# Keys and probabilities turned by VectorE in 32x32 blocks in place of TensorE transposes, in a decoding kernel on one core

## The chip, the core and the metric

The kernel runs on one core of a Trainium2 chip. The metric is the device time of one execution in microseconds (us). The engines that matter: TensorE (PE; its weight loads are PEld), VectorE (DVE), ScalarE (ACT), GpSimd (POOL), and SyncE (SP), whose queue issues nearly all DMA transfers to 16 DMA engines.

## The reference

One decoding step for 8 sequences, width 512. x is normalised (layernorm); the result goes two ways.

```python
q = (xn @ wq).reshape(8, 1, 32, 128)            # 32 query heads, 8 key heads (4 queries each)
k, v = last 2048 positions of k_cache, v_cache  # each batch and key head: 2048 x 128 bf16
p = softmax(q . k * 128 ** -0.5)
s = (p . v).reshape(8, 4096) @ wo
g = silu((sigmoid(xn @ w_gate) * (xn @ w_up)) @ w_down)   # 512 -> 1792 -> 512
out = x + s * g
```

Weights are some 14 MB, keys and values of the window 67 MB; each byte is used once or by four queries.

## The kernel before, in words

All large tensors go through nine slots in SBUF of 16 KB per partition. A list of requests in a fixed order is served first in, first out: `free` gives a slot back and `pump` issues the next transfer on SP's queue. The order is gate, up and down weights (`wd_sb` with 11 rows of w_down on each partition, and a small tile `side` with the 384 rows left, laid on few partitions), wq in two halves, then the cache: one tile for 4 key heads of one batch (2,048 KB, `k_sb` or `v_sb`; a partition holds one head's 64 consecutive positions), the value tiles three places behind the key tiles, and at the end wo in four pieces (16, 10, 4 and 2 of 32 rows). A batch has two key tiles and two value tiles.

The head of the kernel (L194 to L440) computes layernorm, gate and up products, the down product and g, and the queries: `q_ps`, transposed by TensorE (L380), copied to `qm_sb` (L385).

Then a loop over the batches, each in 16 half steps, interleaved by hand through a table `tasks`:

- `k_transposes` (L449): 8 TensorE transposes of 128x128 into PSUM (L456; the identity `perm` also orders the columns by head), then one VectorE copy of 128x1024 to `kT_sb` (L461). 16 of these per batch.
- `scores` (L467): four matmuls, one per head, side by side in strips of 32 columns of the array (L474).
- `row_max` (L485): one VectorE maximum per row of scores (L487), four exponentials with their sums (L494) to `p_buf`. A row holds a quarter of one query's scores.
- `stat_rows`, `factor`, `spread` (L505 to L556): the rows' maxima and sums are turned to one partition, combined into a factor per row, and turned back.
- `p_transposes` (L558): 16 TensorE transposes of the probabilities (L563), two VectorE copies (L568).
- `value` (L574): probabilities times values into `o_ps`; up to batch 4 in the form 128x512, after that 128x256. `values_some` puts them two batches behind the keys.
- `combine`, `normalise`, `turn` (L600 to L639): scaling, and the way back to one column per batch in `oP_sb`.

Behind the loop stands the tail for the last batches, and then the output product: 32 rows of wo, four narrow matmuls each (L706), then two VectorE operations and four small stores. A key slot is freed at its last transpose, a value slot at its last `value`.

What waits on what: SP's queue waits for slots; TensorE takes its instructions in the order written, so a matmul that waits for a tile holds all behind it.

Of the kernel before, what the change touches and what calls it, by code (L numbers as in the profile page):

```python
# [10 lines left out]
def kernel(  # L11
# [30 lines left out]
    CH = CU // 2  # L42
    NU = NQ * NJ
    NR = NU * rep
# [19 lines left out]
        tc.tile_pool(name="ps_t", bufs=4, space=bass.MemoryType.PSUM)  # L64
# [5 lines left out]
        tc.tile_pool(name="ps_o", bufs=1, space=bass.MemoryType.PSUM)  # L70
# [40 lines left out]
    LOW, SF = (5, 5, 3, 3), 15  # L111
    MID, SM = 9, 4
    SP = 4 * max(LOW)
    M_AT = 32
    MP = 4 * MID
    MT = 11
    m0 = MT * P
    m1 = m0 + SF * sum(LOW)
    assert m1 + SM * MP == F
    side = {}  # L120

    def want_side(w, q, at, count, rows, base, of):
        def f(tag=None):
            if tag:
                t = slots.tile([P, SF, w.shape[1]], bf16, name="side", tag=tag)
                nc.gpsimd.memzero(t[:M_AT])  # L126
                side["t"] = t
                rows_of[("side", 0)] = (t, tag)
                for r in range(SF):
                    weights[("wd_sb", MT + r)] = t[: M_AT + MP if r < SM else SP, r]  # L130
            q0.dma_start(  # L131
                out=side["t"][at + q : at + q + 4 * (count - 1) + 1 : 4, :rows].rearrange(
                    "p s n -> p (s n)"
                ),
                in_=w[base : base + of * count * rows, :].rearrange(
                    "(p q s) n -> q p (s n)", q=of, s=rows
                )[q % of],
            )

        todo.append((not side, f))  # L140
        side["asked"] = True
# [32 lines left out]
    sides = []  # L174
    for q in range(4):
        sides.append((q, 0, LOW[q], SF, m0 + q // 2 * 2 * LOW[0] * SF, 2))
        sides.append((q, M_AT, MID, SM, m1, 4))
# [13 lines left out]
    for t0, t1 in ((0, 16), (16, 26), (26, 30), (30, RT)):  # L191
# [13 lines left out]
    perm = consts.tile([P, P], bf16, name="perm")  # L205
    nc.gpsimd.tensor_copy(  # L206
        out=perm[:].rearrange("k (l p) -> k l p", l=G),
        in_=ident[:].rearrange("k (p l) -> k l p", l=G),
    )


    x_f = work.tile([B, D], f32, name="x_f")
    nc.vector.tensor_copy(out=x_f[:], in_=x_bf[:])
    stats = work.tile([B, nc.vector.BN_STATS_DIM], f32, name="stats")
    nc.vector.bn_stats(out=stats[:], in_=x_f[:])
# [7 lines left out]
    xn_bf = work.tile([B, D], bf16, name="xn_bf")  # L223
    nc.vector.tensor_scalar(  # L224
        out=xn_bf[:],
        in0=x_f[:],
# [7 lines left out]
    for kt in range(KT):  # L234
        nc.tensor.transpose(  # L235
            out=xnT_ps[:, kt, :],
            in_=xn_bf[:].rearrange("b (p kt) -> b kt p", kt=KT)[:, kt, :],
            identity=ident[:B, :B],
        )
    xnT_sb = work.tile([P, KT, Z], bf16, name="xnT_sb")  # L240
    nc.vector.memzero(xnT_sb[:])
    nc.vector.tensor_copy(out=xnT_sb[:, :, :B], in_=xnT_ps[:])  # L242
# [5 lines left out]
    h_side = work.tile([B, SF, M_AT + MP], bf16, name="h_side")  # L248
# [4 lines left out]
    M0 = Z - rep  # L253
    qm_sb = work.tile([P, B, Hkv, M0 + Z], bf16, name="qm_sb")
    nc.gpsimd.memzero(qm_sb[:])
    p_buf = [work.tile([P, PG, G, CU], bf16, name=f"p_buf{i}") for i in range(2)]
    for t in p_buf:
        nc.gpsimd.memzero(t[:])
# [16 lines left out]
    for k in range(F // FC):  # L275
        g_ps = ps_t.tile([B, FC], f32, name="g_ps", tag="t")
        for kt in range(KT):
            nc.tensor.matmul(  # L278
                g_ps[:],
                lhsT=xnT_sb[:, kt, :B],  # L280
# [9 lines left out]
    h_bf = ktpool.tile([P, CU * P], bf16, name="h_bf", tag="kT")  # L290
    for k in range(F // FC):
        u_ps = ps_t.tile([B, FC], f32, name="u_ps", tag="t")
        for kt in range(KT):
            nc.tensor.matmul(  # L294
                u_ps[:],
                lhsT=xnT_sb[:, kt, :B],
# [12 lines left out]
    for h in range(2):  # L309
# [10 lines left out]
    nc.gpsimd.tensor_copy(  # L320
        out=h_side[:, :SM, M_AT:],
        in_=h_bf[:B, m1:F].rearrange("b (p t) -> b t p", t=SM),
    )
    cuts = [h_bf[:B, :m0].rearrange("b (p t) -> b t p", t=MT)[:, t] for t in range(MT)]
    rows = [P] * MT + [M_AT + MP] * SM + [SP] * (SF - SM)
    cuts += [h_side[:, t, : rows[MT + t]] for t in range(SF)]
# [5 lines left out]
    for k, t0, t1 in ((M_AT + MP, MT, MT + SM), (SP, MT + SM, MT + SF)):  # L332
        nc.scalar.copy(out=hT_sb[:k, t0:t1, :B], in_=hT_ps[:k, t0:t1])
# [13 lines left out]
    q_ps = [ps_t.tile([P, D], f32, name="q_ps", tag="t") for _ in range(2)]  # L347
    for kt in range(KT):
        for e in range(2):
            for g in range(G):  # L350
                c0 = (G * e + g) * D
                nc.tensor.matmul(  # L352
                    q_ps[e][Z * g : Z * (g + 1), :],
                    lhsT=xnT_sb[:, kt, :],
                    rhs=weights[("wq_sb", kt)][:, c0 : c0 + D],
                    start=(kt == 0),
                    stop=(kt == KT - 1),
                    tile_position=(0, Z * g),
                    skip_group_check=True,
                )  # L360
# [14 lines left out]
    for e in range(2):  # L375
        q_bf = ktpool.tile([P, D], bf16, name="q_bf", tag="kT")
        nc.scalar.mul(out=q_bf[:], in_=q_ps[e][:], mul=scale)
        qT_ps = ps_t.tile([P, rep, G, Z], bf16, name="qT_ps", tag="t")
        for r in range(rep):
            nc.tensor.transpose(  # L380
                out=qT_ps[:, r].rearrange("p g z -> p (g z)"),
                in_=q_bf[:, r * Dh : (r + 1) * Dh],
                identity=ident[:],
            )
        nc.vector.tensor_copy(  # L385
            out=qm_sb[:, :, G * e : G * (e + 1), M0 : M0 + rep].rearrange(
                "p b g r -> p r g b"
            ),
            in_=qT_ps[:, :, :, :B],
        )  # L390
# [13 lines left out]
    for j in range(NB):  # L404
# [12 lines left out]
    Hh = G * rep  # L417
    turn_rows = consts.tile([P, P], bf16, name="turn_rows")
    nc.gpsimd.tensor_copy(
        out=turn_rows[:].rearrange("k (x l r) -> k x l r", x=NU, l=G),  # L420
        in_=ident[:].rearrange("k (l x r) -> k x l r", x=NU, l=G),
    )
    sel_e = consts.tile([P, 2, Hq], f32, name="sel_e")
    for e in range(2):
        nc.vector.reduce_sum(
            out=sel_e[:, e, :].rearrange("k (i h) -> k i h", i=NQ),
            in_=ident_f[:].rearrange(
                "k (i m e h) -> k e i h m", i=NQ, m=NJ // 2, e=2
            )[:, e],
            axis=AX.X,  # L430
        )

    o_ps = ps_o.tile([P, NJ, Dh], f32, name="o_ps")
    sel_j = ident_f[:].rearrange("k (i j h) -> k j i h", i=NQ, j=NJ)
    m_ps = ps_m.tile([P, 512], f32, name="m_ps", tag="m")
    top_ps = m_ps[0:1, 0:P]
    sum_ps = m_ps[0:1, P : 2 * P]
    fac_ps = m_ps[:, 2 * P : 2 * P + 1]
# [3 lines left out]
    kT = {}  # L442
    s_ps = {}
    pT = {}
    st = {}
    row = {}
    fac = {}

    def k_transposes(b, u, h):  # L449
        i, j = u // NJ, u % NJ  # L450
        k_sb = k_tiles[(b, i)][0]
        if h == 0:
            kT[(b, u)] = ktpool.tile([P, CU, P], bf16, name="kT_sb", tag="kT")
        kT_ps = ps_t.tile([P, CH, P], bf16, name="kT_ps", tag="t")
        for c in range(CH):
            nc.tensor.transpose(  # L456
                out=kT_ps[:, c, :],
                in_=k_sb[:, j * CU + h * CH + c, :],
                identity=perm[:],
            )  # L460
        nc.vector.tensor_copy(  # L461
            out=kT[(b, u)][:, h * CH : (h + 1) * CH, :], in_=kT_ps[:]
        )
        if j == NJ - 1 and h == 1:
            free(k_tiles.pop((b, i)))

    def scores(b, u):  # L467
        i, j = u // NJ, u % NJ
        if u == 0:
            s_ps[b] = ps_s.tile([P, CU * PG], f32, name="s_ps", tag="s")  # L470
        t = kT.pop((b, u))
        o = M0 - rep * u
        for l in range(G):
            nc.tensor.matmul(  # L474
                s_ps[b][NR * l : NR * (l + 1), :],
                lhsT=qm_sb[:, b, i * G + l, o : o + Z],
                rhs=t[:, :, PG * l : PG * (l + 1)],
                start=(u == 0),
                stop=(u == NU - 1),
                tile_position=(0, NR * l),  # L480
                skip_group_check=True,
            )


    def row_max(b):  # L485
        st[b] = small.tile([P, 1], f32, name="st")
        nc.vector.tensor_reduce(  # L487
            out=st[b][:], in_=s_ps[b][:], axis=AX.X, op=ALU.max, negate=True
        )
        sums = small.tile([P, 1], f32, name="sums")  # L490
        s = s_ps.pop(b)
        for l in range(G):
            rows = slice(NR * l, NR * (l + 1))
            nc.scalar.activation(  # L494
                out=p_buf[b % 2][rows, :, l, :],
                in_=s[rows, :].rearrange("k (c p) -> k p c", p=PG),
                func=AF.Exp,
                bias=st[b][rows, :],
                accum_out=sums[rows, :],
            )  # L500
        fac[b] = sums

    LI = G * NQ

    def stat_rows(b):  # L505
        nc.tensor.transpose(out=top_ps, in_=st.pop(b)[:], identity=ident_f[:])
        nc.tensor.transpose(out=sum_ps, in_=fac.pop(b)[:], identity=ident_f[:])
        rv = top_ps.rearrange("o (a j r) -> o a j r", a=LI, j=NJ)
        top = small.tile([1, LI, rep], f32, name="top")
        nc.vector.tensor_reduce(  # L510
# [244 lines left out]
```

## Time and profile before

| what | value |
|---|---|
| median of 3 runs | 199.12 us (199.09 to 199.34) |
| profiled execution | 199.33 us |
| its span | 197.5 us, 4796 instructions |
| PE busy | 157.4 us (80%), 2112 matmuls |
| DVE busy | 125.4 us (63%), 245 instructions |
| ACT busy | 40.7 us (21%) |
| POOL busy | 11.0 us (6%) |
| DMA | 81.32 MB, mean 412 GB/s |
| key transposes L456 on PE | 72.6 us |
| their copies L461 on DVE | 84.2 us |

The span is what the profiler saw between the first and the last instruction; the profiled execution's own time is 1.8 us longer. Busy shares are averages over the whole span. In the page's rows of digits, each digit is the busy share of one fortieth of the span in tenths, and 9 means 90% or more. In a group's row stand the line, the engine, the operation, output and input with their shapes, how often, busy time in all, the mean in ns, and the idle time before with what ended it.

### The profile page before, as it was taken

Reading aid. Unit: us, or ns where it says so; the run is one execution under the profiler, and the core shown is the slowest. Engines: PE = TensorE matmul, PEld = TensorE weight load, DVE = VectorE, ACT = ScalarE, POOL = GpSimd, SP = SyncE. Lnnn points to the kernel's source line nnn. Section 1 sums busy time; section 2 is a strip of 40 time slices with the busy share of each in tenths; the row PEclk is TensorE's granted clock in tenths of the full one; section 3 lists DMA queues with packets and bytes.
Section 4 is the critical chain, followed back from the end, with each engine's and each line's share of the span. In section 5 each row is a group of like instructions: output and inputs, shape, how many; then the busy total and the mean of one; then the engine's idle time right before and its main releaser. Section 6 shows DMA issues by size and latency. Waiting matters only on the chain.

```text
span 197.5 us, 4796 instructions
## 1 busy us (share of the span) xinstructions
PE 157.4 (80%) x2112; PEld 103.1 (52%) x2112; DVE 125.4 (63%) x245; ACT 40.7 (21%) x95; POOL 11.0 (6%) x22
## 2 busy tenths in 40 slices
PE   0089559999788898799979987999799979976733
PEld 0034325776664565466545654566466556655531
DVE  4623106999797696679666965796669658935201
ACT  0522022006306001600160016001600160071000
POOL 8910200000000000000000000000000000000000
PEclk9999859999999999999999999999999999999975
DMA  6999999999999999999999999999999999999980
GB/s 205 424 440 435 431 434 435 425 425 431 423 425 425 438 428 435 431 425 428 422 433 431 435 425 433 428 418 428 428 438 431 428 428 431 428 423 425 428 366 21
DMA packets 6396, 81.32 MB, mean 412 GB/s; under 512 B 812, under 2 KB 820, under 8 KB 1624
## 3 DMA queue, kind: packets, MB, share of 16 engines
q1 hardware_dynamic: 6328, 81.01, 96.6%
q8 instruction: 16, 0.26, 0.5%
q10 hardware_dynamic: 48, 0.01, 0.0%
q14 instruction: 4, 0.03, 0.0%
HBM read 81.01 MB, written 0.01 MB: 410 GB/s over the span
## 4 chain that ended last, share of the span: by engine, by line
DMA 73%; PE 22%; POOL 3%; SPq 0%; issue 0%; DVE 0%; POOLq 0%
DMA v_sb<-in_A_v_cache_dram 46%; DMA wo_sb<-in_A_wo_dram 14%; PE kT_ps L456 11%; DMA wq_sb<-in_A_wq_dram 7%; DMA k_sb<-in_A_k_cache_dram 6%; PE o_ps L584 4%; PE s_ps L474 3%; POOL side L126 2%; PE m_ps L614 1%; PE fin_ps L706 1%; PE pT_ps L563 1%; SPq L131 0%; POOL perm L206 0%; POOL hT_sb L245 0%; DVE prod L717 0%
## 5 line engine op out<-in xcount | busy, mean ns | idle before, releaser
L461 DVE COPY kT_sb<-kT_ps 128x1024 bf16<-128x1024 bf16 x128 | 84.2, 683 | 28.9 <-PE kT_ps L456 25.0
L456 PE MATMUL kT_ps<-perm,k_sb 128*128 128x128 bf16 x1024 | 72.6, 220 | 3.7 <-DMA k_sb<-in_A_k_cache_dram 3.7
L456 PEld LDWEIGHTS <-k_sb 128*128 128x128 bf16 x1024 | 58.8, 98 | 26.1 <-issue 16.8
L584 PE MATMUL o_ps<-v_sb,pT_sb 128*32 128x256 bf16 (+1 forms) x352 | 36.5, 327 | 9.0 <-DMA v_sb<-in_A_v_cache_dram 7.6
L474 PE MATMUL s_ps<-kT_sb,qm_sb 128*32 128x512 bf16 x256 | 25.6, 389 | 1.3 <-DVE kT_sb L461 1.1
L494 ACT ACTIVATE p_buf<-s_ps,st 32x512 bf16<-32x512 f32 x32 | 21.7, 679 | 15.4 <-DVE st L487 15.1
L584 PEld LDWEIGHTS <-pT_sb 128*32 128x32 bf16 (+1 forms) x352 | 12.3, 101 | 21.7 <-issue 19.7
L604 ACT ACTIVATE o_sb<-o_ps,fac 128x512 f32<-128x512 f32 (+1 forms) x8 | 4.9, 608 | 60.9 <-PE o_ps L584 60.9
L568 DVE COPY pT_sb<-pT_ps 128x1024 bf16<-128x1024 bf16 x16 | 10.8, 676 | 1.8 <-PE pT_ps L563 1.8
L474 PEld LDWEIGHTS <-qm_sb 128*32 128x32 bf16 x256 | 7.0, 93 | 8.0 <-issue 1.3
L563 PE MATMUL pT_ps<-turn_rows,p_buf 128*128 128x128 bf16 x128 | 10.7, 227 | 0.0
L563 PEld LDWEIGHTS <-p_buf 128*128 128x128 bf16 x128 | 9.4, 149 | 0.2 <-issue 0.2
L521 ACT ACTIVATE w_row<-w 1x128 f32<-1x128 f32 x8 | 2.5, 309 | 30.6 <-DVE w L514 30.6
L235 PE MATMUL xnT_ps<-ident,xn_bf 8*128 8x8 bf16 x4 | 0.3, 176 | 10.6 <-DVE xn_bf L224 10.6
L385 DVE COPY qm_sb<-qT_ps 128x128 bf16<-128x128 bf16 x2 | 1.4, 881 | 8.7 <-PE qT_ps L380 8.7
L301 DVE TENSOR_TENSOR h_bf<-sig,u_ps 8x448 bf16<-8x448 f32 x4 | 2.4, 608 | 6.6 <-PE u_ps L294 6.1
L278 PE MATMUL g_ps<-wg_sb,xnT_sb 128*8 128x448 bf16 x16 | 5.7, 544 | 0.3 <-DVE xnT_sb L242 0.3
L494 ACT ACTIVATION_READ_ACCUMULATOR p_buf<-s_ps,st 32x1 f32 x32 | 5.9, 184 | 0.0
L706 PE MATMUL fin_ps<-wo_sb,oP_sb 128*32 128x128 bf16 x128 | 3.3, 263 | 3.1 <-DMA wo_sb<-in_A_wo_dram 3.1
L487 DVE TENSOR_REDUCE st<-s_ps 128x1 f32<-128x512 f32 x8 | 5.4, 681 | 0.5 <-PE s_ps L474 0.5
L235 PEld LDWEIGHTS <-xn_bf 8*128 8x128 bf16 x4 | 0.2, 117 | 10.6 <-DVE xn_bf L224 10.6
L352 PE MATMUL q_ps<-wq_sb,xnT_sb 128*32 128x512 bf16 x32 | 3.1, 526 | 3.2 <-DMA wq_sb<-in_A_wq_dram 3.2
(88 smaller groups left out, 92.0 us busy)
## 6 DMA issues: line engine op xcount, KB each, us to landing
k_sb<-in_A_k_cache_dram SPq DMA_DIRECT2D x16, 2048.0 KB
v_sb<-in_A_v_cache_dram SPq DMA_DIRECT2D x16, 2048.0 KB
wq_sb<-in_A_wq_dram SPq DMA_DIRECT2D x2, 2048.0 KB
wo_sb<-in_A_wo_dram SPq DMA_DIRECT2D x1, 2048.0 KB
wg_sb<-in_B_w_gate_dram SPq DMA_DIRECT2D x2, 896.0 KB
wu_sb<-in_B_w_up_dram SPq DMA_DIRECT2D x2, 896.0 KB
wd_sb<-in_B_w_down_dram SPq DMA_DIRECT2D x1, 1408.0 KB
wo_sb<-in_A_wo_dram SPq DMA_DIRECT2D x1, 1280.0 KB
```

Of the source, the lines that this page charges most:

```text
L126: nc.gpsimd.memzero(t[:M_AT])
L278: nc.tensor.matmul(g_ps[:], lhsT=xnT_sb[:, kt, :B], rhs=weights[("wg_sb", kt)][:, k * FC : (k + 1) * FC], start=(kt == 0), stop=(kt == KT ...
L456: nc.tensor.transpose(out=kT_ps[:, c, :], in_=k_sb[:, j * CU + h * CH + c, :], identity=perm[:],)
L461: nc.vector.tensor_copy(out=kT[(b, u)][:, h * CH : (h + 1) * CH, :], in_=kT_ps[:])
L474: nc.tensor.matmul(s_ps[b][NR * l : NR * (l + 1), :], lhsT=qm_sb[:, b, i * G + l, o : o + Z], rhs=t[:, :, PG * l : PG * (l + 1)], start=(u ...
L487: nc.vector.tensor_reduce(out=st[b][:], in_=s_ps[b][:], axis=AX.X, op=ALU.max, negate=True)
L494: nc.scalar.activation(out=p_buf[b % 2][rows, :, l, :], in_=s[rows, :].rearrange("k (c p) -> k p c", p=PG), func=AF.Exp, bias=st[b][rows, ...
L563: nc.tensor.transpose(out=pT_ps[:, c, :], in_=p_buf[b % 2][:, :, :, h * CH + c].rearrange("k p l -> k (p l)"), identity=turn_rows[:],)
L568: nc.vector.tensor_copy(out=pT[b][:, h * CH : (h + 1) * CH, :], in_=pT_ps[:])
L584: nc.tensor.matmul(o_ps[r] if b < WIDE else o_ps[r, 0:2], lhsT=pT[b][:, c, r], rhs=x, start=(c == 0), stop=(c == CU - 1), tile_position=(0 ...
L604: nc.scalar.activation(out=o[:, :n], in_=o_ps[:, :n], func=AF.Copy, scale=fac.pop(b)[:])
L706: nc.tensor.matmul(fin_ps[Z * j : Z * (j + 1), :], lhsT=oP_sb[:, t, :], rhs=weights[("wo_sb", t)][:, j * P : (j + 1) * P], start=(t == 0), ...
```

## The change

- Keys: TensorE's transposes and the copies out of PSUM go. `k_turn` lets VectorE transpose a quarter of a key tile in place, in blocks of 32x32 pairs of bf16 (seen as 4-byte elements), and writes each block so that the eight pairs of one head stand together. 8 turns per batch in place of 16 copies.
- Scores: `q_wide` holds the queries spread over a 128-row pattern with zeros (filled by GpSimd in `widen` for every batch, with two buffers). 16 matmuls of full height, 512 columns, per key tile; keys are read with a step of one pair. A row now belongs to a query and a part of the positions. The key tile is freed after its scores.
- Softmax: `row_max` transposes the rows' maxima to one partition, `head_max` takes one maximum for each query and spreads it back by a matmul; four exponentials over all 128 rows, each with a mask that leaves one head; `factor` is one matmul, one sum and one reciprocal.
- Probabilities: turned by VectorE (`p_turn`), from `p_buf` to `pT_sb`.
- Values: 16 matmuls of 64 rows by 512 columns per value tile, all batches alike; two buffers of `o_ps`.
- The queries' projection uses the whole array, and VectorE turns the queries.
- The down weights: 13 rows on each partition, `side` holds 128 rows in pieces of 4 KB.
- The output product: the first 16 rows of wo in wide matmuls of 512 columns, copied by ScalarE and added with `fold` before row 26; the rest as before.

The core of the diff:

```diff
-    def k_transposes(b, u, h):
...
-        for c in range(CH):
-            nc.tensor.transpose(
-                out=kT_ps[:, c, :],
-                in_=k_sb[:, j * CU + h * CH + c, :],
-                identity=perm[:],
-            )
-        nc.vector.tensor_copy(
-            out=kT[(b, u)][:, h * CH : (h + 1) * CH, :], in_=kT_ps[:]
-        )
+    def k_turn(b, s):
+        i, j = s // NJ, s % NJ
+        x = (
+            k_tiles[(b, i)][0][:, j * CU : (j + 1) * CU, :]
+            .rearrange("p c d -> p (c d)")
+            .bitcast(f32)
+        )
+        nc.vector.transpose(
+            out=x.rearrange("p (c l h) -> p c h l", l=G, h=2 * NA), in_=x
+        )
...
+    def scores(b, i):
...
+        for n in range(NW // NQ):
+            j, l, e = n // (2 * G), n // 2 % G, n % 2
+            o = (i * (NW // NQ) + n) * P + M0 - NL * i - rep * l
+            nc.tensor.matmul(
+                s_ps[b][:],
+                lhsT=q_wide[b % 2][:, o : o + P],
+                rhs=k[:, j, l, e],
...
+        free(k_tiles.pop((b, i)))
...
+    def exps(b):
...
+        for l in range(G):
+            nc.scalar.activation(
+                out=p_buf[b][:, :, :, l, :],
+                in_=s[:].rearrange("k (c e) h -> k c h e", e=2),
+                func=AF.Exp,
+                bias=bias[:, l : l + 1],
+                scale=mask[:, l : l + 1],
+                accum_out=sums[b][:, l : l + 1],
+            )
+
+    def p_turn(b):
+        pT[b] = ppool.tile([P, NQ, CT // 2, NL, 2], bf16, name="pT_sb")
+        nc.vector.transpose(
...
-    LOW, SF = (5, 5, 3, 3), 15
-    MID, SM = 9, 4
+    LOW, SF, SH = (5, 5, 3, 3), 8, 4
...
-    MT = 11
+    MT = 13
...
     for b in range(B):
+        tasks = {s: [] for s in range(NS)}
         if b >= 1:
+            tasks[0].append(lambda: scores(b - 1, 1))
+            tasks[1].append(lambda: row_max(b - 1))
+            tasks[2].append(lambda: head_max(b - 1))
+            tasks[2].append(lambda: exps(b - 1))
+            tasks[6].append(lambda: p_turn(b - 1))
+            tasks[6].append(lambda: factor(b - 1))
+        tasks[0].append(lambda: widen(b))
+        tasks[4].append(lambda: scores(b, 0))
...
+        for s in range(NS):
+            k_turn(b, s)
             for f in tasks[s]:
                 f()
...
     scores(last, 1)
     combine(last - 2)
     row_max(last)
+    values(last - 1, 0, 4)
+    head_max(last)
+    exps(last)
     normalise(last - 2)
+    values(last - 1, 4, NN)
+    turn(last - 2)
     combine(last - 1)
+    p_turn(last)
+    factor(last)
...
+    RG = 16
+    f_ps = ps_t.tile([P, D], f32, name="f_ps", tag="t")
+    for t in range(RG):
+        g = slice(Z * (t % G), Z * (t % G + 1))
+        nc.tensor.matmul(
+            f_ps[g, :],
+            lhsT=oP_sb[:, t, :],
+            rhs=weights[("wo_sb", t)],
...
+    nc.scalar.copy(out=f_sb[:], in_=f_ps[:])
+    for t in range(RG, RT):
+        if t == 26:
+            fold(fin_ps, f_sb, False, False)
```

The whole program has 4,091 instructions on TensorE's queue before and 1,464 after.

## The prediction

> **What bounds the kernel now.** I read the slices first, then the transfer queues, the chain, the groups of instructions, and last the end of the span in windows and in order of time.
>
> ```profile
> PE   0089559999788898799979987999799979976733
> DVE  4623106999797696679666965796669658935201
> DMA  6999999999999999999999999999999999999980
> q1 hardware_dynamic: 6328, 81.01, 96.6%
> q8 instruction: 16, 0.26, 0.5%
> DMA 73%; PE 22%; POOL 3%; SPq 0%; issue 0%; DVE 0%; POOLq 0%
> ```
>
> The DMA row is 9 from the second slice to the last but one: 81.01 MB move at some 428 GB/s from about 3 us to 191 us, whatever the engines do. The chain agrees (DMA 73%). So an engine's saving counts only where it changes when the stream ends, what follows the stream, or where an engine falls so far behind that slots come free late. One cache tile (2,048 KB) takes 2.097 MB / 428 GB/s = 4.9 us, a batch (four tiles) 19.6 us; that is the pace every engine must hold. The end, in windows (columns: length, PE, PEld, DVE, ACT, POOL busy, clock, DMA share, GB/s):
>
> ```profile
> 188.00:190.00 2.00, 1.08 (x64) 1.02 (x65) 0.03 (x1) 0.00 (x0) 0.00 (x0) 1.00 1.02 430
> 190.00:191.00 1.00, 0.00 (x0) 0.00 (x0) 0.00 (x0) 0.00 (x0) 0.00 (x0) 0.63 0.77 320
> 191.00:192.00 1.00, 0.14 (x8) 0.14 (x11) 0.00 (x0) 0.00 (x0) 0.00 (x0) 0.50 0.86 342
> 192.00:193.00 1.00, 1.00 (x40) 0.92 (x33) 0.00 (x0) 0.00 (x0) 0.00 (x0) 0.50 0.56 217
> ```
>
> The same in order of time:
>
> ```profile
> 188.81 1.08 PE L706 MATMUL fin_ps<-wo_sb,oP_sb 128*32 128x128 bf16 x64 [1.12 <-DMA wo_sb<-in_A_wo_dram]
> 191.86 2.28 PE L706 MATMUL fin_ps<-wo_sb,oP_sb 128*32 128x128 bf16 x64 [1.97 <-DMA wo_sb<-in_A_wo_dram]
> 194.19 0.29 DVE L717 TENSOR_TENSOR prod<-gg_sb,fin_ps 128x128 f32<-128x128 f32 x1 [6.16 <-PE fin_ps L706]
> ```
>
> The share falls raggedly from 190 us: some of the 16 DMA engines are done while others work to 193.2 us. PE waited for wo at 188.81 and 191.86, at a granted clock of 0.50 the second time; matmuls end at 194.1.
>
> **The stream.** Bytes stay: wd grows from 1,408 to 1,664 KB, side shrinks from 384 KB (2 x 75, 4 x 36, 2 x 45) to 128. What goes is code: in the built order of instructions PE has 4,091 rows before and 1,464 after. The 16 instruction packets above are 0.5% of 16 engines' span, 0.005 x 16 x 197.5 = 15.8 us, some 1 us each; 16 for 4,091 rows makes 6 for 1,464. Ten fewer save 10 us / 16 = 0.6 us per DMA engine: last landing 192.6 instead of 193.2. Which engine carries which packet and side row decides the ragged edge; the windows show some 1 us lost there, so I allow 0.6 us either way.
>
> **Slots.** A key slot is freed after the scores instead of after the transposes, half a tile later; a value slot comes free one or two eighths of a batch earlier. Counting the requests against nine slots, a transfer's slot is free some 15 to 20 us before the queue reaches it (key tile 6 takes the slot of key tile 0, free near 39 us, and is due near 69). Hidden; it costs only if an engine falls 15 us behind.
>
> **VectorE per batch.** Removed: 16 copies L461, 2 copies L568, seven small row operations. Added: 8 turns of 128x1024 4-byte elements, one turn of P, a maximum over 512 elements on one partition, small ones.
>
> ```profile
> L461 DVE COPY kT_sb<-kT_ps 128x1024 bf16<-128x1024 bf16 x128 | 84.2, 683 | 28.9 <-PE kT_ps L456 25.0 <-PE m_ps L632 3.4
> L487 DVE TENSOR_REDUCE st<-s_ps 128x1 f32<-128x512 f32 x8 | 5.4, 681 | 0.5 <-PE s_ps L474 0.5
> L639 DVE CAST oP_sb<-m_ps 128x32 bf16<-128x32 f32 x7 | 2.0, 292 | 0.6 <-PE m_ps L632 0.6
> L556 DVE COPY fac<-m_ps 128x1 f32<-128x1 f32 x8 | 1.1, 138 | 0.6 <-PE m_ps L550 0.6
> ```
>
> No turn of this kind is in the trace. L487 against L556 gives (681 - 138) / 511 = 1.06 ns per 4-byte element, so a turn at that pace is 1024 x 1.06 + 0.1 = 1.2 us. The other end is L639: it writes 2-byte elements 64 bytes apart and takes (292 - 138) / 31 = 5.0 ns per element; the key turn writes 4-byte words 32 bytes apart, so at worst 1024 x 5.0 + 0.1 = 5.2 us. Nothing excludes either end. I take 1.2 us: L639 writes half words, the turn whole ones, and L331, which writes runs of 16 bytes at 64-byte steps, pays nothing (88 elements, 202 ns). Per batch 8 x 1.2 + 1.2 + 0.68 + 0.65 + five small ones 1.0 = 13.1 us, under 19.6.
>
> [...]
>
> **TensorE per batch.** Gone: 128 key transposes (72.6 us in all) and 16 of P (10.7). Scores become 32 full-height 512-column matmuls, one after the other; the nearest row is L294, 16 of 448 columns in 3.19 us, 0.2 each, 0.23 for 512: 7.3 us. Values: 32 of the 128*64 form, 26.8 / 160 = 0.167 each: 5.3 us. With some 1 us of small ones 13.6 us, under 19.6. The moving keys are read with 4-byte steps, of which no row tells; the bounds are 0.23 and twice that (21 us per batch, too slow); I take 0.23, since every 512-column row here lies nearer to it.
>
> **ScalarE and GpSimd.** Exponentials stay 4 per batch over 512 columns: L494 (0.68 + 0.18, one each 0.79 us in the timeline), 3.2 us. They now write pairs, 4 bytes, 16 bytes apart: between 0.79 and, at 5.0 ns per pair, 256 x 5.0 + 0.35 = 1.6 us each. I take 0.79. GpSimd spreads the queries, 4 copies of at most 0.47 us (L206) per batch, beside everything.
>
> **The tail.** Here compute meets the stream. The last key tile is there at 164.5 us, V tiles 13, 14, 15 near 174.1, 179.0, 183.9 (188.8 less 4.9 each). Four turns to 169.3; scores 3.7 to 173.0; maximum 0.7; PE does four steps of values(6), which need V 13, to 175.4; head maximum and bias to 175.9; exponentials 3.2 to 179.1; turn of P 1.2 to 180.3; value(7,0) 16 x 0.23 to 184.0; normalise 0.6; value(7,1) 3.7 to 188.3 (before: 185.9); combine 0.7 to 189.0; normalise to turn 1.65, as before, to 190.6; 16 wide output matmuls, four at a time at 0.33 (L474), 1.3 to 191.9; 40 narrow ones at 1.08 / 64 = 0.017, 0.7, to 192.6; fold 0.43 (L337) to 193.0; 24 narrow ones 0.4 to 193.4. The stream's own end: 192.6 + 0.5 to the waiting PE + 0.15 = 193.3. Both give 193.4 in place of 194.1: 0.7 us less. The clock fell in the window in which PE stood idle (0.63); with the change PE does not stand idle there, so I take full clock; at half clock (the 2.28 against the 1.08 us above) the last 64 steps cost 1.2 us more.
>
> **Sum.** The profiled execution took 199.33 us, its span is 197.5, and the median of the runs is 199.12. 199.33 - 0.7 = 198.6; taken from the median 198.4. The tail has no margin, so I keep the upper value: **198.6 us**.
>
> **Rivals.**
> 1. Scattered writes bind VectorE. Place: the key turn. The first can start at 32.5 us, and 60 turns and seven batches of 3.5 us of other work must be done when the last tile lands: 32.5 + 60x + 24.5 = 164.5, x = 1.8 us. From there each 0.1 us costs 6.4 us. At L639's pace (5.2 us): 32.5 + 64 x 5.2 + 24.5 + 27 of tail = 417 us; at twice the contiguous pace (2.3 us) 231. For: L639 and L385 (128 scattered elements, 0.88 us). Against: both are half-word writes. Chance 0.14.
> 2. The tail's compute comes out late: exponentials at 1.6 us put 3.2 us ahead of value(7,0), of which 0.1 us is hidden, or the clock stays at 0.50. End at 194.6 to 196.5 in place of 194.1; 199.8 to 201.7 us. For: no slack in the sum. Against: wide rows of ACT are all 0.59 to 0.69 us. Chance 0.20.
> 3. It does nothing: the code's packets were not on the last DMA engine, or the new side rows are. The stream ends at 193.2: 199.1 us. Chance 0.16.
> 4. Forecast: 197.8 to 198.9, chance 0.50.
>
> What a measurement can tell from no change is about 0.2% (0.4 us). Faster: 4 but its upper edge, with the luckier part of 3, 0.50; same 0.17; slower 0.33. The range is 197.8 to 201.8: it leaves out rival 1, whose bounds reach to 417, and little below.
>
> **What would show it.** DMA row of 9 throughout and q8 with about 6 packets: the stream step. A key turn at 1.2 us on VectorE: right; over 1.8 us and a DMA row with holes: rival 1. Exponentials at 0.8 or 1.6 us, and whether PE's last matmuls wait for wo_sb or for oP_sb: rival 2. A ragged end as long as now: rival 3.

## The result, and the profile after

The changed kernel took 238.56 us (median of 4 runs, 237.07 to 238.97) against 199.13 us (199.09 to 199.34) for the kernel before in the same session: a ratio of 1.1964, 95% interval 1.1912 to 1.2016. The forecast was 198.6 us, in a range of 197.8 to 201.8. The profiled execution took 238.57 us, its span is 236.8 us. Here and below, medians and ranges hold all executions of a kernel, while ratios and their intervals leave out those that took over 1.5% longer than its fastest.

The slices of the span after (PE, DVE, the granted TensorE clock, DMA), the queue of the code, and the chain's shares by engine:

```profile
PE   0098940862861994985499559955995599578974
DVE  5614049998999988849594959496949684623000
PEclk9999995697799798598759875987598759889997
DMA  6999999999999999999999999599849994500000
q8 instruction: 6, 0.10, 0.1%
PE 56%; DVE 38%; issue 2%; ACT 1%; DMA 1%; DVEq 0%; ACTq 0%
```

Before, the chain was 73% DMA and the DMA row was full to the end. Now DMA holds 1% of the chain, and its row has holes from the 26th slice on: slots come free late. No engine is at 9 throughout in its place. PE shows 9955, DVE 9594, over and over, and the clock falls in every round (9875): a pattern with a period of four slices, 24 us. The chain of waits, in order of time (start, length, engine, tile, line, count), shows one such round:

```profile
108.97 5.32 PE s_ps L478 x16
114.31 0.69 DVE st L489
115.01 1.89 DVE k_sb L465
...
118.42 1.88 PE m_ps L598 x8
120.30 5.40 PE s_ps L478 x16
125.69 1.85 PE o_ps L570 x16
...
127.70 0.30 DVE oP_sb L623
128.00 1.81 DVE k_sb L465
129.81 1.06 DVE pT_sb L543
...
131.12 1.89 DVE k_sb L465
...
133.05 5.32 PE s_ps L478 x16
```

From one score row to the same row of the next batch it is 133.05 - 108.97 = 24.1 us, where the stream delivers a batch in 19.6. In this round VectorE is busy 18.1 us and TensorE 17.6: each has room, but they take turns. Two places in the written order show in the chain. `row_max` (L489) stands at half step 1, right behind `scores` of the same tile at half step 0; VectorE waits there, 12.5 us in all, with all its turns queued behind. And `turn` of an older batch (its copy L623) stands at half step 5: its matmul is on TensorE's queue behind `scores` of half step 4 and the values, so VectorE waits again, 20.9 us in all, while the next `scores` wait for the turns behind that copy. A third is smaller: `normalise` (L598) waits on TensorE for the bias of `head_max` (2.5 us in all), ahead of the next `scores`. Now the three groups of instructions that the forecast priced:

```profile
L465 DVE STREAM_TRANSPOSE k_sb<-k_sb 128x1024 f32<-128x1024 f32 x64 | 121.4, 1971 | 0.0
L478 PE MATMUL s_ps<-k_sb,q_wide 128*128 128x512 bf16 x256 | 80.0, 479 | 32.4 <-DVE k_sb L465 21.3
L532 ACT ACTIVATE p_buf<-s_ps,bias,mask 128x512 bf16<-128x512 f32 x32 | 25.3, 812 | 99.3 <-DVE bias L516 99.3
```

A key turn takes 1.97 us, not 1.2; 0.77 us more, 64 times. A score matmul takes 5.32 / 16 = 0.33 us in the ring, against the 0.23 assumed. The exponentials start 0.78 us after each other, against the 0.79 assumed. The windows of one round show at which clock the matmuls ran (length, PE, PEld, DVE, ACT, POOL, clock, DMA share, GB/s):

```profile
106.00:109.00 3.00, 0.30 (x5) 0.12 (x2) 2.97 (x5) 0.69 (x1) 0.00 (x0) 1.00 1.01 431
109.00:114.00 5.00, 5.00 (x16) 1.81 (x15) 3.54 (x2) 0.00 (x0) 0.00 (x0) 0.66 1.00 429
```

TensorE stood nearly idle for 3 us, and the next 5 us of scores were granted 0.66 of the clock: in steps of 1 us, 1.00 from 109 us, 0.65 from 110, and 0.50 from 111 to 113. Behind the loop there is a long tail: the last key turn ends at 204.9 us, and 32 us of mostly serial work follow, in which DMA moves next to nothing.

### The profile page after: what moved, and what is told of

Same layout as the page of the kernel before. It is cut to its first block, busy times and chain, and to the rows that moved or that the text cites. A ratio compares the mean times of both kernels' runs of the same rounds, so it can differ in the third digit from the quotient of the medians.

```text
span 236.8 us, 2156 instructions
## 1 busy us (share of the span) xinstructions
PE 158.9 (67%) x833; PEld 73.8 (31%) x834; DVE 157.9 (67%) x151; ACT 40.7 (17%) x87; POOL 21.2 (9%) x53
## 4 chain that ended last, share of the span: by engine, by line
PE 56%; DVE 38%; issue 2%; ACT 1%; DMA 1%; DVEq 0%; ACTq 0%
PE s_ps L478 29%; DVE k_sb L465 24%; PE o_ps L570 9%; PE m_ps L598 5%; DVE pT_sb L543 3%; PE q_ps L337 3%; PE g_ps L268 3%; DVE x_f L202 2%; DVE st L489 2%; PE m_ps L508 2%; DVE low L499 1%; PE u_ps L284 1%; DVE oP_sb L623 1%; DMA x_bf<-in_A_x_dram 1%; PE f_ps L681 1%
## 5 line engine op out<-in xcount | busy, mean ns | idle before, releaser
L465 DVE STREAM_TRANSPOSE k_sb<-k_sb 128x1024 f32<-128x1024 f32 x64 | 121.4, 1971 | 0.0
L478 PE MATMUL s_ps<-k_sb,q_wide 128*128 128x512 bf16 x256 | 80.0, 479 | 32.4 <-DVE k_sb L465 21.3
L478 PEld LDWEIGHTS <-q_wide 128*128 128x128 bf16 x256 | 29.1, 116 | 79.8 <-issue 65.4
L532 ACT ACTIVATE p_buf<-s_ps,bias,mask 128x512 bf16<-128x512 f32 x32 | 25.3, 812 | 99.3 <-DVE bias L516 99.3
L570 PE MATMUL o_ps<-v_sb,pT_sb 128*64 128x512 bf16 x256 | 34.3, 382 | 0.6 <-DVE fac L560 0.6
L371 POOL COPY q_wide<-qT 32x128 bf16<-32x128 bf16 x32 | 12.8, 400 | 116.4 <-PE s_ps L478 114.9
L570 PEld LDWEIGHTS <-pT_sb 128*64 128x64 bf16 x256 | 14.8, 109 | 14.9 <-issue 2.5
L623 DVE CAST oP_sb<-m_ps 128x32 bf16<-128x32 f32 x7 | 2.1, 296 | 20.9 <-PE m_ps L616 20.9
L489 DVE TENSOR_REDUCE st<-s_ps 128x1 f32<-128x512 f32 x8 | 5.5, 692 | 12.8 <-PE s_ps L478 12.5
L508 PE MATMUL m_ps<-one,low 1*128 1x1 f32 x16 | 4.1, 326 | 14.6 <-DVE low L499 14.6
L598 PE MATMUL m_ps<-ident_f,o_sb 128*128 128x32 f32 x56 | 11.6, 365 | 2.5 <-DVE bias L516 2.5
L598 PEld LDWEIGHTS m_ps<-ident_f,o_sb 128*128 128x128 f32 x56 | 10.8, 289 | 3.2 <-issue 3.2
L543 DVE STREAM_TRANSPOSE pT_sb<-p_buf 128x1024 f32<-128x1024 f32 x8 | 9.7, 1217 | 0.0
L202 DVE CAST x_f<-x_bf 8x512 f32<-8x512 bf16 x1 | 5.6, 5583 | 2.7 <-DMA x_bf<-in_A_x_dram 2.7
```

Source lines behind the costliest of these rows:

```text
L202: nc.vector.tensor_copy(out=x_f[:B], in_=x_bf[:])
L371: nc.gpsimd.tensor_copy(out=t[g, : NW * P].rearrange("p (i x e c) -> p i x e c", i=NQ, x=2 * G, e=2)[:, :, :, :, M0 + Z * a : M0 + Z * a + ...
L465: nc.vector.transpose(out=x.rearrange("p (c l h) -> p c h l", l=G, h=2 * NA), in_=x)
L478: nc.tensor.matmul(s_ps[b][:], lhsT=q_wide[b % 2][:, o : o + P], rhs=k[:, j, l, e], start=(i == 0 and n == 0), stop=(i == NQ - 1 and n == ...
L489: nc.vector.tensor_reduce(out=st[b][:], in_=s_ps[b][:].rearrange("k c h -> k (c h)"), axis=AX.X, op=ALU.max,)
L508: nc.tensor.matmul(all_ps, lhsT=low[:].rearrange("o a x -> o (a x)"), rhs=one[:], start=True, stop=True,)
```

## The experiments

Three theories. **A**: the scattered write makes the turn long, and VectorE is the bound. **B**: TensorE's full-height scores at half clock are the bound (**B2**: only because they stand in the ring). **C**: the order is the bound, since it makes VectorE and TensorE wait for each other in a ring.

### The write without a step (e1)

```diff
-        nc.vector.transpose(
-            out=x.rearrange("p (c l h) -> p c h l", l=G, h=2 * NA), in_=x
-        )
+        nc.vector.transpose(out=x, in_=x)
```

The scores read as before, so the heads are mixed in this kernel and in e6 below.

> The key turn writes its blocks densely; the scores read as before, so the kernel mixes heads and its output is not the reference's; everything else is unchanged. Theory A (the scattered write of the turn is the cause): a turn falls from 1.97 to about 1.2 us, VectorE keeps pace with the stream of 19.6 us per batch, time 199 to 204 us. Theory B (TensorE's full-height scores, at half clock, are the bound): two scores of 5.3 us and 10 us of other work per batch stay, time 215 us or more. Theory C (VectorE and TensorE wait for each other in a ring of 24.0 us per batch): four of the eight turns lie on the ring, 24.0 - 4 x 0.77 = 20.9 us per batch, time 208 to 214 us.

210.03 us (209.93 to 210.79), ratio 1.0544 (1.0526 to 1.0562). The turn took 1219 ns. The round in the chain fell from 24.1 to 20.5 us (score rows at 117.53 and 138.06), still above 19.6, and VectorE still waited 29.9 us for `turn` and 14.6 us for `row_max`. So the write's price is real, and without it the ring and the tail still cost 11 us: C's number, not A's. C's sum had four turns on the ring, but the chain has three, which save 3 x 0.75 = 2.3 of the 3.6 us; the rest fits the clock, since one of the round's two rows of scores is back at 3.64 us, while the other takes 5.8.

### The order alone, then the tail (e4, e5)

e4 keeps the scattered write and moves small steps, so that neither engine waits for what the other was only just given:

```diff
-            tasks[1].append(lambda: row_max(b - 1))
-            tasks[2].append(lambda: head_max(b - 1))
-            tasks[2].append(lambda: exps(b - 1))
-            tasks[6].append(lambda: p_turn(b - 1))
-            tasks[6].append(lambda: factor(b - 1))
...
+            tasks[2].append(lambda: normalise(b - 3))
+            tasks[3].append(lambda: turn(b - 3))
...
+            tasks[2].append(lambda: factor(b - 2))
...
+            tasks[2].append(lambda: row_max(b - 1))
+            tasks[3].append(lambda: head_max(b - 1))
+            tasks[3].append(lambda: exps(b - 1))
+            tasks[7].append(lambda: p_turn(b - 1))
...
-            tasks[3].append(lambda: normalise(b - 3))
-            tasks[5].append(lambda: turn(b - 3))
```

> Scattered writes as in the changed kernel; only the order of the small steps is different: maximum and normalising one or two turns later, the way to oP_sb ahead of the scores, the turn of P at the end of the batch, the factor a batch later, so that VectorE waits less for TensorE. A: turns of 1.97 us stay, VectorE's own work of 8 x 1.97 + 3.7 = 19.5 us per batch is no faster than the ring by much, 225 to 238 us. C: VectorE's waits of some 4 us per batch go, 24.0 falls to about 20 us, time 210 to 220 us. B: no change.

e5 also writes the tail in another order: the turn of the last probabilities ahead of an older copy, and the last batch's values in pairs instead of one tile after the other (16 in 1.92 us in the loop, 3.64 us singly in the tail).

> The order of the fourth run, and a tail in which the last batch's values run as pairs of both halves (16 pairs in 3.7 us, as the pairs of the loop did, in place of two rows of 16 single ones of 3.7 us) and the turn of P no longer waits for oP_sb. Scattered writes stay. Theory C (ring, and a tail that is serial by its order): 4.9 us less than the fourth run's 210.4, 205 to 206 us. Theory A alone (only the turn's duration counts): no change against the fourth run, 209 to 211 us.

e4 took 210.36 us (208.96 to 211.43), ratio 1.0558 (1.0497 to 1.0619): the order alone is worth 28 us, with the turn still at 1965 ns. It moves several steps at once, and what each of them is worth was not taken apart. e5 took 206.31 us (206.2 to 208.4), ratio 1.038 (1.0329 to 1.0431). The chain of e5, by engine:

```profile
DVE 69%; PE 23%; ACT 3%; issue 2%; DMA 1%; ACTq 0%; DVEq 0%
```

With the ring gone, VectorE is the bound by itself. One of its batches in the chain of e5, from `row_max` to `row_max`:

```profile
109.44 0.59 DVE st L489
...
113.31 7.43 DVE k_sb L465 x4
...
128.24 0.59 DVE st L489
```

A batch takes it 18.8 us, under the stream's 19.6, but it begins 33.9 us in and has to work off what has landed; its last turn ends at 177.1 us, 13 us after the last key tile could be there (164.5 in the prediction). Back to back, turns start every 7.43 / 4 = 1.86 us or less, although each is listed with 1.97.

This is the first rival of the prediction. Its sum gives 32.5 + 64 x 1.97 + 24.5 + 27 = 210.1 us, and e4 measured 210.4, but that is luck: the sum has the last turn end at 183.1 us and 27 us of tail behind it, while in e4 the last turn ends at 177.4 us and 32.2 us follow.

### Both taken away (e6)

e5 with the write of e1.

> The fifth run's order and tail with dense writes as in the first run (heads are mixed, as there). If scattered writes, ring and tail together are all that was missed, the last key tile is turned near 170 us as in the kernel before, and the time is 198 to 201 us. If something else holds the changed kernel back (TensorE at half clock, theory B), it stays at 203 us or more.

198.15 us (197.82 to 203.18, 10 runs), ratio 0.9974 (0.9943 to 1.0005). The slices of DMA, the turns, and the end of the span in order of time:

```profile
DMA  6999999999999999999999999999999999999990
L465 DVE STREAM_TRANSPOSE k_sb<-k_sb 128x1024 f32<-128x1024 f32 x64 | 74.4, 1215 | 31.4 <-DMA k_sb<-in_A_k_cache_dram 31.4
```

```profile
191.79 0.41 PE L693 MATMUL fin_ps<-wo_sb,oP_sb 128*32 128x128 bf16 x16 [0.30 <-DMA wo_sb<-in_A_wo_dram]
192.41 0.29 PE L693 MATMUL fin_ps<-wo_sb,oP_sb 128*32 128x128 bf16 x8 [0.21 <-DMA wo_sb<-in_A_wo_dram]
192.75 0.29 DVE L704 TENSOR_TENSOR prod<-gg_sb,fin_ps 128x128 f32<-128x128 f32 x1 [3.47 <-PE fin_ps L693]
```

VectorE waits for keys from DMA, TensorE's last matmuls wait for wo, and the last product starts at 192.75 us (194.19 before; 193.4 was forecast). So with a write without a step, another order and another tail, the stream is the bound again (DMA has 54% of the chain), as the prediction had it, and the time is the one it gave. It is not the kernel of the prediction: that order and tail, with the turn at the price that was assumed, are e1, at 210.03 us. How the 11.9 us between e1 and e6 part between order and tail was not measured. Theory B is out: a row of scores still takes up to 6.39 us here, at a granted clock of 0.56 (82.85 to 89.24 us), and the stream does not wait for it. Whether e6 is faster than the kernel before can't be told from its interval.

### What a step costs, for the writer and for the reader (e2, e3, e7)

The turn may write with a smaller step if the scores then read what lies closer together. Only the two patterns change:

```diff
-            out=x.rearrange("p (c l h) -> p c h l", l=G, h=2 * NA), in_=x
+            out=x.rearrange("p (c l h) -> p c h l", l=G, h=2), in_=x
...
-            "p c (j l h e) -> p j l e c h", j=2, h=2 * NA, l=G
+            "p c (j a l h e) -> p j l e c a h", j=2, a=4, h=2, l=G
```

This is e3 (a write step of 8 bytes); e2 writes without a step and e7 with 16 bytes; all put each head where it belongs.

> The turn writes densely, and the scores' matmuls read keys with a step of 16 bytes instead of 4, so that the right heads meet. A: turn 1.2 us as in the run with dense writes, and the same time if the moving operand's step costs nothing. If the step costs as much as it costs VectorE's writes, a score matmul rises from 0.23 to about 0.4 us at full clock, 16 of them to 6.4 us, and the time stays at 215 us or more. B expects 215 us or more in any case.

> The turn writes with a step of 8 bytes (two pairs of one head stand together) instead of 32; the scores read two pairs, 8 bytes, and skip 24. A: if the price comes with each change of a 16-byte piece, half the writes pay, turn 1.4 to 1.6 us; if it comes with any step beyond one element, 1.97. Time then between the run with dense writes and 238 us, about 205 to 215 us. C: ring of 24.0 less 4 x 0.4 to 0.8 us per batch, 210 to 225 us.

> The turn writes with a step of 16 bytes (four pairs of one head together), the scores read runs of 16 bytes. If the price is one for each 16-byte piece that a run of writes or reads enters (1 piece per element: 1.97 us per turn at 32 bytes; 0.5 per element: 1.22 us at 8 bytes; for the matmuls 128 pieces 0.23, 256 pieces 0.44, 512 pieces 0.87 us), then here the turn takes 1.97 us and a score matmul 0.23 us at full clock, and the time is that of the changed kernel, 236 to 241 us. If the price grows with the step, the turn takes 1.4 to 1.7 us, and the time is 220 to 232 us.

e2 took 373.53 us (ratio 1.8761), e3 250.67 us (ratio 1.2548, 1.2461 to 1.2635), e7 237.84 us in its only execution. e7 came out as expected; e3 missed its 205 to 225 us, and e2's score matmuls took 0.87 us, where some 0.4 was expected. Their turns and scores in the groups, e2, e3 and e7:

```profile
L476 PE MATMUL s_ps<-k_sb,q_wide 128*128 128x512 bf16 x256 | 222.5, 1036 | 16.9 <-DVE k_sb L465 9.4
L465 DVE STREAM_TRANSPOSE k_sb<-k_sb 128x1024 f32<-128x1024 f32 x64 | 75.6, 1219 | 0.0
```

```profile
L478 PE MATMUL s_ps<-k_sb,q_wide 128*128 128x512 bf16 x256 | 113.3, 610 | 17.0 <-DVE k_sb L465 9.4
L465 DVE STREAM_TRANSPOSE k_sb<-k_sb 128x1024 f32<-128x1024 f32 x64 | 75.6, 1220 | 0.0
```

```profile
L465 DVE STREAM_TRANSPOSE k_sb<-k_sb 128x1024 f32<-128x1024 f32 x64 | 121.4, 1972 | 0.0
```

The write: 1.22 us without a step and with 8 bytes, 1.97 us with 16 and with 32. So each word cost (1971 - 1219) / 1024 = 0.73 ns more where it lay in another piece of 16 bytes than the word before it, and no more for the larger step; where two words shared a piece, they cost nothing more. The reader paid sooner. Busy time over 256 gives 0.87 us per score matmul where each 16-byte piece gives one of its 512 columns (e2) and 0.44 us where it gives two (e3); where it gives four, 16 scores took 3.64 us at full clock (e8), 0.23 each. Per piece that is 1.7 to 1.8 ns in all three. The clocks were not the same, but with one or two columns per piece they hardly count: e3's matmuls take 0.44 us at a granted clock of 1.00 (46 to 52 us) and of 0.50 (68 to 72 us) alike, and e2's rows of 16 take 13.9 us at 0.50 (71 to 85 us) as at a mean of 0.68 (125 to 139 us). No row of e2 ran at full clock from end to end. As long as the four heads lie interleaved on the partitions, writer or reader has to step, and both ways cost more than the forecast had.

### The clock (e8)

The changed kernel with 12 matmuls more per batch (512 columns, their result is not read), six at each of two places where TensorE waits:

```diff
+            tasks[0].append(lambda: warm(6))
...
+            tasks[1].append(lambda: warm(6))
```

> The changed kernel with 12 more matmuls of 512 columns per batch, whose result nobody reads, at the two places where TensorE waits for VectorE (ahead of the second scores and behind the transposed maxima). Nothing else is changed. Theory B2 (the half clock in the ring is what makes a turn's delay so dear): the granted clock stays at 0.95 or more, 16 scores take 3.65 us in place of 5.3, the ring falls from 24.0 to about 20.5 us, time 208 to 215 us. If the clock is not at the root: the added work lies in the ring, 24 us or more per batch, time 238 to 250 us.

223.92 us (223.44 to 229.56), ratio 1.1231 (1.1209 to 1.1254), 14.6 us less with more work on TensorE, and between the two expectations. The granted clock in its slices:

```profile
PEclk9999995579669969999999999999999999799988
```

From the 17th slice on it is full almost to the end of the loop, a score row takes 3.64 us, and the round 20.4 us (128.44 to 148.85 in the chain) in place of 24.1. That is B2's round, but not its time: before the 17th slice the clock still falls, and the tail stays at 32 us. So the half clock lengthened the ring, and the ring's waits lowered the clock; it was not the bound by itself, since 25 us are still lost.

### Looking for a version with the heads in place (e9, e10, e11)

All three have e5's order. They let the heads come from memory in an order in which the turn needs no costly step. e9 loads a key tile by four transfers of 32 partitions:

```diff
+                src = rows.rearrange("l (a h c) d -> a l h (c d)", a=PG // B, c=CT)
+                for a in range(PG // B):
+                    q0.dma_start(
+                        out=t[Z * a : Z * (a + 1)].rearrange("p c d -> p (c d)"),
+                        in_=src[a],
+                    )
```

> The order and the tail of e5, the dense write of e6, and each head where the scores want it: a key tile is loaded by four transfers of 32 partitions each in place of one of 128, so that the four heads lie interleaved on the partitions and the turn needs no scattered write. Nothing of the computation is left out. If all that separated the changed kernel from the forecast was the turn's duration, the order's ring and the tail, this gives the time of e6, 197.5 to 199 us (ratio 0.992 to 1.000), with turns of 1.22 us, score matmuls as in e6 and a full DMA row. Rival: a transfer of 32 partitions does not keep all DMA engines busy, or the heads' rows collide, and the stream runs under 428 GB/s: 205 us or more, with a DMA row of 8s or less and PE and VectorE waiting for k_sb from the queue throughout.

e10 by two of 64, in which every second partition is filled:

> As e9, with the key tile loaded by two transfers of 64 partitions instead of four of 32: the heads lie interleaved in pairs of partitions, and the turn writes pairs of 4-byte words, 8 bytes together, so that two writes fall into each 16-byte piece and the scores find whole runs of 32 bytes. Nothing is left out. In e9 each transfer had 4 rows in its outer dimension and the stream ran at some 109 GB/s in the loop, a quarter of 428, as if 4 of the 16 DMA engines worked; here the outer dimension is 16. If the number of engines goes by the outer dimension, the stream is back at 428 GB/s, the turn takes 1.22 us as in e3, a score matmul as in e6, and the time is that of e6, 197.5 to 199 us (ratio 0.992 to 1.000). Rival 1: it goes by the partitions, eight to an engine; then 64 partitions give half rate, 214 GB/s on the keys, and 290 us or more. Rival 2: the pattern of four free dimensions costs VectorE more than 1.22 us per turn; from about 1.9 us it is e5 again, 206 us.

e9 took 509.0 us (ratio 2.5541), e10 297.77 us (274.36 to 314.97, 6 executions; the profile is of the longest). The rates in GB/s in e9's slices, and e10's queue and rates:

```profile
GB/s 344 418 109 108 107 156 146 125 178 108 192 108 178 124 151 152 112 190 110 197 105 179 124 146 155 108 195 107 196 107 167 133 137 223 288 216 212 122 110 52
```

```profile
GB/s 293 435 432 270 230 232 211 226 331 222 318 229 324 216 314 216 308 220 306 211 291 222 293 213 264 217 242 216 225 228 211 224 211 193 247 322 431 407 145 21
q1 hardware_dynamic: 6544, 81.01, 96.0%
```

In e9, whose transfers have 4 in their outer dimension, the keys move at 108 GB/s, a quarter of 428, and the mean busy share of the 16 engines is 0.26 where 110 GB/s move (26 to 50 us). In e10, with 16 in the outer dimension, 96% of the engines' span is busy, yet the keys move at about half rate, 210 to 230 GB/s. That is the rate of e10's first rival, but not its reason, since all engines work. Whether the number of engines goes by the outer dimension, as e10's expectation asked, was not shown: the two runs differ in more than that. Why each of them is half as fast in this layout, where a transfer fills every second partition, was not settled.

e11 loads each head by itself, 16 positions on a partition in pieces of 4 KB:

```diff
-                in_=cache[b, G * i : G * (i + 1), win0:Sk, :].rearrange(
-                    "l (p c) d -> p l (c d)", c=CT
-                ),
+                    in_=rows.rearrange("l (p c) d -> p l (c d)", c=CU),
...
+                in_=s[:]
+                .rearrange("k c h -> k (c h)")
+                .rearrange("k (c h e q) -> k q c h e", e=2, h=2 * NA, q=2),
...
+            rhs=v_tiles[(b, i)][0][:].rearrange("p (e c) d -> p c e d", e=2)[
+                :, 2 * n : 2 * n + 2
+            ],
```

> The order and the tail of e5, the dense write of e6, and each head by itself: a key tile is loaded by one transfer in which a partition holds 16 positions of each of the four heads (pieces of 4 KB) in place of 64 positions of one head (16 KB). So a turned block holds 32 positions of one head, the turn writes without a step, and the scores read runs of 128 bytes. The positions' new order is taken up by the exponentials (they read PSUM with a step of 2 in place of 8) and by the value matmuls (positions c and c + 32 make a pair). Nothing is left out. Expected, if the turn, the order and the tail were all that parted the changed kernel from the forecast: 197.5 to 199 us (ratio 0.992 to 1.000), as e6, with a DMA row of 9s, turns of 1.22 us, score matmuls of 0.23 and exponentials of 0.8 us. Rival: pieces of 4 KB move slower than those of 16 KB. Each 10% on the keys' 33.6 MB would cost 8 us: 206 us and more, with a full DMA row and less than 428 GB/s. Second rival: the changed read of the exponentials doubles them, 0.8 to 1.6 us; it would be hidden in the loop and cost some 3 us in the tail, 201 us.

199.89 us (199.64 to 201.78, 10 runs), ratio 1.0052 (1.0028 to 1.0077). Its turns take 1215 ns, its exponentials 804 ns, its DMA row is full: the costly step is gone, with the heads in place, and with the order and the tail of e5 38.7 of the 39.4 us are back. It missed the 197.5 to 199 us that were expected, and is still 0.5% slower than before, and 1.7 us behind e6. In its profiled execution (201.68 us) the last key turn ends at 169.7 us (167.9 in e6) and the last product starts at 196.62: the tail's compute comes out last, behind keys that came some 2 us later. But this is one of its longer executions and e6's profile is of its shortest, so the distance between the two traces (3.9 us) is more than that of the medians. The keys' pieces of 4 KB are one candidate for the cause, the values' changed read (393 ns per matmul, 381 in e6) another; no run took them apart. None of the versions is shown to beat the kernel before.

## Why the prediction was wrong, point by point

- **The failed step** is the one that set each engine's busy time per batch beside the stream's 19.6 us ("13.1 us, under 19.6" for VectorE, "13.6 us, under 19.6" for TensorE) and took both as hidden. Even the true sums, 18.1 and 17.6 us in a round, are under 19.6. What counts is the path through both engines in the written order, 24.1 us. e4 changed that order alone and won 28 us; and e1, with the turn at the price that was assumed and the order as it stood, still took 210.03 us, outside the range. The path could have been walked before: the new order of half steps was in the diff, and it shows `row_max` directly behind its scores and VectorE's copy in `turn` behind TensorE's `scores`.
- **The turn**, taken at 1.2 us of a range of 1.2 to 5.2, took 1.97. The step had the right direction in L639 and the wrong size from it: 5.0 ns per half word there, 0.73 ns more per word here. L331, the row that seemed to speak against a cost, wrote 16 bytes together. In the runs VectorE's write cost nothing more at steps of 8 bytes (1.22 us) and did at 16 (1.97); TensorE's read at full clock still took 0.44 us at two columns per piece, against 0.23 at four. The write without a step came at the pace that was assumed: 1219 ns for 1024 elements, where the prediction had 1.2 us.
- **Rival 1** had the right place, the key turn, and its signs came (over 1.8 us, a DMA row with holes). But it priced only VectorE: at 1.97 us its sum gives 210.1, not 238.6, and where the ring was gone (e4) the sum was near by two errors that cancel.
- **Full clock** was taken for the tail because "with the change PE does not stand idle there", and for the scores of the loop without a word on the clock. In the loop TensorE was idle two or three times in each round, and the score rows ran at 5.3 in place of 3.64 us; e8 puts this at 14.6 us. The last score row, in the tail, took 5.32 us too.
- **The tail** was summed for work that begins when the last key tile lands: 24.1 us from the last turn (169.3) to the last product (193.4). In the changed kernel the last turn ends at 204.9 and the last product starts 28.6 us later, at 233.5. The 192.75 of e6 is no proof of the sum: there the values run in pairs, and at the end TensorE waits for wo.
- **The costs overlap.** Of the 39.4 us the write alone takes 28.5 (e1), the order alone 28.2 (e4), the clock alone 14.6 (e8). They share the same ring: a shorter turn, or shorter scores, shortens the round until the stream's 19.6 us take over. Taken one after the other they are 28.2 (order), 4.1 (tail) and 8.2 us (write), 40.4 in all, which leads from 238.56 to 198.15.
- **Right** were the stream's bytes and code (q8 has 6 packets, as counted), the exponentials (one each 0.78 us against 0.79), the turn of the probabilities (1.22 against 1.2), and the score matmul at full clock (0.23).

## What to carry to other kernels

When work moves from one engine to another, don't compare busy sums with the bound one engine at a time: write down, for one round of the loop, who waits for whom in the order of each queue, and add up that path, where TensorE waits in it also at a lower clock (here 5.3 us for a row of scores in place of 3.64). Dependent steps placed right behind their producer on another engine's queue held all that was queued after them here (VectorE waited 12.5 us at `row_max` and 20.9 at `turn`); moving such steps, most of them by one or two half steps, was worth as much here as taking the step out of the write (28.2 and 28.5 us, each alone). Before a write or read with a step is priced, count how many of its elements fall into one 16-byte piece: here that parted turns of 1.22 us from 1.97, and score matmuls of 0.23 us from 0.44 and 0.87.

## What the hardware showed that was not expected

- VectorE's turn of 1024 4-byte words took 1.97 us at steps of 16 and of 32 bytes alike, and 1.22 at 8 as without a step. A score matmul that moves 512 columns took 0.23 us at full clock with four columns from each 16-byte piece, 0.44 with two at full and half clock, 0.87 with one at mean clocks of 0.50 to 0.68.
- ScalarE's exponentials, which now write 4 bytes at steps of 16, take 0.81 us each and 0.68 before, but start at the same distance (0.78 and 0.79 us), since each now begins 0.09 us before the sum of the one ahead of it is read out. Rows and reading pattern changed too, so the step's own price is not known.
- After a wait of 2.7 us on TensorE (106.27 to 108.97) the clock was still full for over 1 us, then fell to 0.50; and matmuls whose result nobody reads made the kernel 14.6 us faster. Busy is not enough, though: in e2 the clock stood at 0.50 from 41 to 66 us with TensorE busy all the time, on reads that give one column per piece.
- Key transfers with 4 in their outer dimension moved 108 GB/s with a quarter of the engines' time busy (e9). All 16 engines busy is no full rate either: some 220 GB/s with every second partition filled (e10).
- The first cast of x took 5.58 us in place of 2.61 (L202 after, L213 before), and the first turn started at 34.6 us, not 32.5. In both kernels the cast ends 0.3 us behind a long GpSimd memset (`side` until 5.07 us before, `q_wide` until 7.99 after), and in the traces of e1, e4, e6, e8, e9 and e11 it ends at the same 8.3 us, whether it began at 2.2 or 3.5. So the new memsets are the likely cause, but no run took them away.
